# Ninth half rows of two weight matrices laid on the lower 64 partitions, in transfers of eight partitions

## The chip, the core and the metric

The kernel runs on one core of one Trainium2 chip. The metric is the device time of one execution in microseconds (us). Three runs of the kernel before took 2691.22, 2691.80 and 2693.41 us; their median is 2691.8 us. One further execution was profiled.

## The reference

The reference decodes one token for a batch of two through four blocks: attention, gated MLP, attention, gated MLP, each with a layer norm before it and the residual added after it. Both attention blocks use the same weights and the same cache, and so do both MLP blocks.

```python
# x (2, 1, 576); H = 32 heads, 8192 cached positions, head size 128; gate and up 576 x 4608
q = (ln(x) @ wq).reshape(B, 1, H, 128)
scores = einsum("bhqd,bhkd->bhqk", q, k_cache) * 128 ** -0.5
x = x + (einsum("bhqk,bhkd->bhqd", softmax(scores), v_cache)) @ wo
x = x + (gelu(ln(x) @ w_gate) * (ln(x) @ w_up)) @ w_down
# ... and both once more
```

All values are float32. The key and value caches are 268 MB each and are read once per attention block, apart from what the first block leaves in SBUF; `wq` is 9.4 MB, `w_gate` and `w_up` are 10.6 MB each.

## The kernel before, in words

**Items.** An attention block goes through 64 items: 60 pairs of heads of one batch entry, and four single heads. The keys of a pair lie on 128 partitions, 64 KB on each, and come as one transfer; so do its values. VectorE multiplies keys by the query (L554), GpSimd adds the two halves of each product (L574), VectorE sums the rest (L577), and TensorE multiplies the softmax weights with the values (L670). Block 0 goes up through the items, block 1 comes back down.

**Memory.** All keys, values and weights lie in one SBUF tile, `space`, 50,176 floats on each partition. `Arena` places them when the program is written. `plan_first`, `plan_mlp` and `plan_second` put the loads in one fixed list, and `pump` emits a load as soon as its place in the arena is free. All these loads are issued by one queue, SP, in that order, so a load that waits holds back all behind it.

**Counters.** The layer that turns the kernel into a program gives the transfers eight completion counters in turn. A transfer that takes a counter is not issued before the former transfer on the same counter has landed, so no more than eight are under way. It also puts a wait where a transfer writes to a part of a tile that an earlier instruction still uses.

**Half rows.** `wq`, and the gate and up matrices of the second MLP, are read by half rows. A matrix of 576 rows has 1152 half rows; partition p holds the nine half rows 9p to 9p+8, so a transfer of three of them is one run in DRAM on each partition. A half row of `wq` is 8192 bytes, one of the gate matrix 9216. The first `wq` and the second gate each come as three transfers of three half rows (`three`, L293). `norm` makes the matching left operand: one transpose on VectorE (L487) writes to `xt`, which has 32 columns for each of the nine half rows; TensorE then multiplies `xt` with `w` (L505 for `wq`, L843 for gate and up), one group of matmuls for each half row.

**The start.** SP issues the three transfers of the first `wq`, then K0 (the keys of the first pair), K1 and V0. The input `x` comes in eight small transfers of two partitions each from the queue of ScalarE (L140). The first multiplication on VectorE needs q, thus all of `wq`, and K0.

**The end.** After the last value products SP issues the eight transfers of `wo`, three of the gate matrix, five of the up matrix and seven of the down matrix; the last down products and the output store follow.

Of the kernel before, what the change touches and what calls it, by code (L numbers as in the profile page):

```python
# [9 lines left out]
F32 = mybir.dt.float32  # L10
# [5 lines left out]
P = 128  # L16
B = 2
H = 32
SK = 8192
DH = 128  # L20
# [5 lines left out]
HALF = P // 2  # L26

GH = 4
NU = 9
EQ = 512  # L30
HG = DF // 16
PAD = 6
# [8 lines left out]
NPLACE = 4  # L41
RING = 5 * SLOT
END = RING + NPLACE * PLACE
HELD = 5


# [21 lines left out]
class Arena:  # L68
# [38 lines left out]
    def fit(self, key, n, lo=0):  # L107

        for at in [self.at, lo] + sorted(end for _, end in self.live.values()):
            if lo <= at and at + n <= END and self.take(key, at, n) is not None:  # L110
                self.at = at + n
# [11 lines left out]
def decode_layers(ctx, tc, x_in, kc, vc, wq, wo, wg, wu, wd, out):  # L123
    nc = tc.nc
    scale = DH ** -0.5

    consts = ctx.enter_context(tc.tile_pool(name="consts", bufs=1))
    work = ctx.enter_context(tc.tile_pool(name="work", bufs=2))
    once = ctx.enter_context(tc.tile_pool(name="once", bufs=1))
    psum1 = ctx.enter_context(tc.tile_pool(name="psum1", bufs=1, space=PSUM))  # L130
    ctx.enter_context(tc.manual_schedule())

    space = consts.tile([P, END], F32, name="space")

    x = consts.tile([P, CW], F32, name="x")
    nc.vector.memset(x, 0.0)
    for c in range(4):
        for s in range(2):
            lo = 32 * c + s * B
# [69 lines left out]
    def weights(key, n, first, transfers):  # L209

        def make():
            at = arena.ring(key, n) if first is None else arena.fit(key, n, first)
            if at is None:
                return False
            t = ready[key] = part_at(at, n)
            transfers(t)
            return True

        queue.append(make)

    def half_rows(key, w, us, first):

        width = w.shape[1] // 2
        rows = w.rearrange("r (s w) -> (r s) w", w=width).rearrange("(p u) w -> p u w", p=P)

        def transfers(t):
            nc.sync.dma_start(t.rearrange("p (u w) -> p u w", w=width), rows[:, us[0]:us[-1] + 1, :])

        weights(key, len(us) * width, first, transfers)

    def split_rows(name, w, h, u):

        rows = w[:, DF // 2 * h:DF // 2 * (h + 1)].rearrange("(m r) w -> m r w", r=NU)

        def transfers(t):
            for e in range(2):
                nc.sync.dma_start(t[e::2, :], rows[:, 5 * e + u, :])

        weights((name, 0, h, u), DF // 2, None, transfers)
# [51 lines left out]

    single = [range(u, u + 1) for u in range(NU)]
    three = [range(u, u + 3) for u in range(0, NU, 3)]  # L293
    WQ = [three, single]
    GU = [three, three[:-1] + single[-3:]]

    DOWN = [
        [[(t, i) for i in range(lo, lo + 4)] for t in range(NT) for lo in (0, 4)] + [[(t, NI - 1) for t in range(NT)]],
# [12 lines left out]
    def plan_first():  # L311
        def k(n, *at):
            cache(name("k", 0, n), kc, n, *at)

        def v(n, *at):
            cache(name("v", 0, n), vc, n, *at)

        for us in WQ[0]:
            half_rows(("wq", 0, us[0]), wq, us, END - NU * H * DH // 2)
        last = PAIRS - 1  # L320
        k(0)
        for n in range(1, PAIRS):
            k(n)
            v(n - 1)
        k(SINGLE[0], (0,))
        half(("v", 0, last), vc, last, 0, 1)
        half(("v", 0, last), vc, last, 4, 5)
        k(SINGLE[1], (3,))
        v(SINGLE[0], (4,))

        k(SINGLE[2], (2,))
        products()
        k(SINGLE[3], (0,))
        v(SINGLE[1], (4,))
        v(SINGLE[2], (3,))
        for g in groups(0)[:2]:
            out_rows(0, g)
        v(SINGLE[3], (1,), (1,) * 4)
        for g in groups(0)[2:]:
            out_rows(0, g)  # L340
# [34 lines left out]
    def plan_mlp(layer):  # L375
        if layer == 0:
            for h in range(2):
                for u in range(4):
                    split_rows("g", wg, h, u)
                split_middle(h)  # L380
                for u in range(4):
                    split_rows("u", wu, h, u)
        else:
            for g, (name, w) in enumerate((("g", wg), ("u", wu))):
                for us in GU[g]:
                    half_rows((name, layer, us[0]), w, us, 0)
        for rows in DOWN[layer]:
            down(layer, rows)

# [20 lines left out]
    diag = consts.tile([P, 4], F32, name="diag")  # L410
    of = consts.tile([P, B], F32, name="of")
    both = ident.rearrange("p (c v b r) -> p b r v c", c=4, v=4, b=B)[:, :, :, 0, :]
    eight = consts.tile([P, B, 4], F32, name="eight")
    nc.vector.reduce_sum(eight, both, axis=AX.X)
    nc.vector.tensor_add(diag, eight[:, 0, :], eight[:, 1, :])
    nc.vector.reduce_sum(of, eight, axis=AX.X)
# [18 lines left out]

    xt = consts.tile([P, PAD + NU * 32], F32, name="xt")
    nc.vector.memset(xt, 0.0)


    acc = psum1.tile([P, 2, 512], F32, name="acc")
# [16 lines left out]
        return smalls[0][0:p, 0:n]  # L459


    def norm(split=False):
        stats = work.tile([P, 6], F32, name="stats")
        nc.vector.bn_stats(stats, x)
        apart = work.tile([P, 4, 6], F32, name="apart")
        nc.vector.tensor_mul(
            apart, stats.unsqueeze(1).to_broadcast([P, 4, 6]), strip.unsqueeze(2).to_broadcast([P, 4, 6])
        )
        every4 = small(P, 4 * 6)
        nc.tensor.matmul(every4, same, apart.rearrange("p c t -> p (c t)"), start=True, stop=True)  # L470
        mv = work.tile([P, 2], F32, name="mv")
        nc.vector.bn_aggr(mv, every4)
        xc = once.tile([P, CW, 2], F32, name="xc", tag="xc")
        xr = x.rearrange("p (m r) -> p r m", r=NU)
        xs = xc.rearrange("p w s -> p (w s)")
        if split:
            xm = xs[:, :5 * 32].rearrange("p (u m e) -> p u m e", u=5, e=2)
            parts = [(xm[:, 0:4, :, e], xr[:, 5 * e:5 * e + 4, :], 0) for e in range(2)]
            parts += [(xm[:, 4, :, e], xr[:, 4, :], e) for e in range(2)]
            xs = xs[:, :5 * 32].rearrange("p (u q) -> p u q", u=5)  # L480
        else:
            parts = [(xc[:, :, s], x, s) for s in range(2)]
            xs = xs.rearrange("p (q u) -> p u q", u=NU)
        for to, of_x, s in parts:
            nc.vector.tensor_scalar(to, of_x, mv[:, 0:1], side[:, s:s + 1], op0=ALU.subtract, op1=ALU.mult)
        u = xs.shape[1]
        nc.vector.transpose(xt[:, PAD:PAD + 32 * u].rearrange("p (u q) -> p u q", u=u), xs)  # L487
        ve = work.tile([P, 1], F32, name="ve")
        nc.vector.tensor_scalar_add(ve, mv[:, 1:2], EPS)  # L489
        rstd = work.tile([P, 1], F32, name="rstd")  # L490
        nc.gpsimd.tensor_tensor(out=rstd, in0=ve, in1=mhalf, op=ALU.pow)  # L491
        return rstd
# [3 lines left out]


    def attention(layer):
        rstd = norm()

        for us in WQ[layer]:
            w = ready.pop(("wq", layer, us[0])).rearrange("p (u c w) -> p u c w", c=4, w=EQ)
            for u in us:
                for c in range(4):
                    nc.tensor.matmul(  # L505
                        acc[32 * c:32 * c + 2 * B, 0, :], xt[:, PAD + 32 * u:PAD + 32 * u + 2 * B],
                        w[:, u - us[0], c, :], start=(u == 0), stop=(u == NU - 1),
                    )
            done(("wq", layer, us[0]))
        qsb = once.tile([P, EQ], F32, name="qsb", tag="row")  # L510
# [231 lines left out]
        for i, n in enumerate(seq):  # L742
            last = i == N - 1
            p = seq[i - 1] if i else None

            v = {N - 2: None, N - 1: N - 3}.get(i, i - 1) if layer == 0 else i - 1
# [3 lines left out]
            first = layer == 1 and i == 1  # L750
# [39 lines left out]
        n, p = seq[-1], seq[-2]  # L790
        add_up(n, ITEMS[n].parts - 1)
        first, second = groups(layer)[:2]
# [17 lines left out]

    def mlp(layer):
        split = layer == 0
        rstd = norm(split)
        hT = once.tile([P, 2, NI, 2, 2, B], F32, name="hT", tag="xc")

        def window(u, at):

            return xt[:, PAD + 32 * u - at:PAD + 32 * u - at + 4 * B]
# [16 lines left out]
        def all_products():  # L835

            for g, name in enumerate("gu"):
                for us in GU[g]:
                    w = ready.pop((name, layer, us[0])).rearrange("p (u v c w) -> p u v c w", v=2, c=4, w=HG)
                    for u in us:  # L840
                        for v in range(2):
                            for c in range(4):
                                nc.tensor.matmul(  # L843
                                    acc[32 * c:32 * c + 4 * B, v, :HG], window(u, 4 * g), w[:, u - us[0], v, c, :],
                                    start=(g == 0 and u == 0), stop=(g == 1 and u == NU - 1),
                                )
                    done((name, layer, us[0]))
# [25 lines left out]
        for rows in DOWN[layer]:  # L873
            w = ready.pop(("d", layer, rows[0])).rearrange("p (i c) -> p i c", c=D)
            for k, (t, i) in enumerate(rows):
                v, e = divmod(t, 2) if split else (t % 2, t // 2)
                for c in range(4):
# [3 lines left out]
                        start=(rows is DOWN[layer][0] and k == 0), stop=(t, i) == (NT - 1, NI - 1),  # L881
# [39 lines left out]
```

## Time and profile before

| What | Value |
|---|---|
| median of three runs | 2691.8 us (2691.22 to 2693.41) |
| profiled execution | 2693.42 us |
| its span | 2691.6 us |
| moved by DMA | 1154.36 MB, mean 429 GB/s |
| busy: VectorE, GpSimd, TensorE, ScalarE | 69%, 45%, 34%, 5% of the span |

The profiled execution's own time is 1.8 us more than its span, and 1.6 us over the median. The profile gives a line for each queue of the DMA engines (q1 is SP's, q10 ScalarE's, q8 and q14 fetch instructions), the chain of work that ended last, and on request the busy share of the 16 DMA engines and the bytes per second in any stretch of time. A stretch counts a packet's time and bytes in the slice where the view puts the packet, so a short stretch can show a share over 1.

### The profile page before, as it was taken

To read this page: it belongs to the slowest core of one execution; us is meant where nothing else is said; L and a number is where in the kernel's file an instruction comes from. 1 tells how busy PE (TensorE), PEld (TensorE's weight loads), DVE (VectorE), ACT (ScalarE), POOL (GpSimd) and SP (SyncE) were. 2 spreads that over 40 slices of the span, in tenths; PEclk is the share of its full clock that TensorE was granted. 3 is DMA by queue.
4 is the path that set the end of the run, shared out by engine and by line. 5 is a ranking of instruction groups with operands and counts; after the bars stand their busy time and mean duration, and the time that the engine had idled before them with its cause. 6 is when DMAs were issued, how large, how long until landed. Compare 5 with 4: busy or idle time off the path is not lost.

```text
span 2691.6 us, 18179 instructions
## 1 busy us (share of the span) xinstructions
PE 919.8 (34%) x7020; PEld 302.3 (11%) x7020; DVE 1850.8 (69%) x1688; ACT 145.6 (5%) x736; POOL 1213.8 (45%) x550
## 2 busy tenths in 40 slices
PE   1323332333233233334554232233233323332355
PEld 0100010000001010111211110001000100010022
DVE  4877787678677776867028777768767867787740
ACT  0000000000000000000016000000000000000000
POOL 2644454455445444544018554445444544454420
PEclk7656655665666566666756665666566556656667
DMA  9999999999999999999999999999999999999998
GB/s 421 436 435 434 433 431 435 429 435 434 432 435 433 434 433 429 433 429 426 407 397 416 435 434 436 434 430 436 430 433 434 435 432 433 436 433 430 430 426 374
DMA packets 33687, 1154.36 MB, mean 429 GB/s; under 512 B 4008, under 2 KB 4032, under 8 KB 5824
## 3 DMA queue, kind: packets, MB, share of 16 engines
q1 hardware_dynamic: 33560, 1153.19, 99.6%
q8 instruction: 55, 0.90, 0.1%
q14 instruction: 32, 0.26, 0.0%
q10 hardware_dynamic: 40, 0.01, 0.0%
HBM read 1153.18 MB, written 0.00 MB: 428 GB/s over the span
## 4 chain that ended last, share of the span: by engine, by line
DMA 79%; PE 12%; DVE 7%; POOL 1%; issue 1%; ACT 0%; SPq 0%; ACTq 0%; POOLq 0%; DVEq 0%
DMA space<-in_A_k_cache_dram 40%; DMA space<-in_A_v_cache_dram 32%; PE acc L670 10%; DVE space L554 4%; DMA space<-in_B_w_down_dram 2%; DVE S L577 2%; DMA space<-in_B_w_gate_dram 2%; DMA space<-in_A_wo_dram 1%; DMA space<-in_B_w_up_dram 1%; POOL space L574 1%; DMA space<-in_A_wq_dram 1%; PE bank L878 0%; PE acc L829 0%; POOL space L561 0%; DMA x<-in_A_x_dram 0%
## 5 line engine op out<-in xcount | busy, mean ns | idle before, releaser
L574 POOL TENSOR_TENSOR space<-space 128x1024 f32<-128x1024 f32 (+1 forms) x510 | 1180.7, 2315 | 1206.1 <-DVE space L554 1195.3
L554 DVE TENSOR_TENSOR space<-space,bank 128x2048 f32<-128x2048 f32 (+1 forms) x512 | 1153.6, 2253 | 604.7 <-DMA space<-in_A_k_cache_dram 576.5
L670 PE MATMUL acc<-space,prz 128*8 128x512 f32 x4096 | 594.3, 744 | 454.5 <-DMA space<-in_A_v_cache_dram 450.4
L577 DVE TENSOR_REDUCE S<-space 128x16 f32<-128x1024 f32 (+1 forms) x512 | 609.6, 1191 | 3.2 <-POOL space L574 3.0
L525 PE MATMUL bank<-qsb,pick 4*64 4x128 f32 (+1 forms) x256 | 47.0, 439 | 777.9 <-DVE space L554 765.6
L670 PEld LDWEIGHTS acc<-space,prz 128*8 128x8 f32 x4096 | 118.5, 104 | 873.4 <-DMA space<-in_A_v_cache_dram 452.7
L629 ACT ACTIVATE nbs<-bank 64x1 f32<-64x1 f32 (+1 forms) x128 | 21.2, 165 | 2258.6 <-PE bank L608 2257.7
L525 PEld LDWEIGHTS bank<-qsb,pick 4*64 4x64 f32 (+1 forms) x256 | 21.1, 203 | 836.7 <-DVE space L554 794.3
L695 PE MATMUL bank<-of,osb 128*32 128x2 f32 x512 | 40.9, 202 | 130.9 <-DVE osb L686 130.9
L608 PE MATMUL bank<-m,unit 1*128 1x2 f32 (+1 forms) x136 | 39.2, 355 | 129.5 <-DVE m L606 129.5
L491 POOL TENSOR_TENSOR rstd<-ve,mhalf 128x1 f32<-128x1 f32 x4 | 2.2, 550 | 168.6 <-DVE ve L489 168.6
L686 DVE SCALAR_TENSOR_TENSOR osb<-acc,diag,osb 128x128 f32<-128x128 f32 x192 | 67.3, 351 | 6.8
L640 PE MATMUL bank<-sums,unit 128*128 128x2 f32 x120 | 35.2, 363 | 92.2 <-ACT prz L631 92.2
L854 DVE STREAM_TRANSPOSE o<-o 128x288 f32<-128x288 f32 x4 | 2.8, 689 | 91.8 <-ACT o L852 91.8
L631 ACT ACTIVATE prz<-S,nbs 64x128 f32<-64x128 f32 (+1 forms) x128 | 50.7, 396 | 12.4 <-POOL prz L621 8.3
L695 PEld LDWEIGHTS bank<-of,osb 128*32 128x32 f32 x512 | 35.7, 154 | 139.1 <-DVE osb L686 137.9
L608 PEld LDWEIGHTS bank<-m,unit 1*128 1x128 f32 x136 | 33.3, 303 | 149.2 <-DVE m L606 149.2
L600 PE MATMUL bank<-ident,m 128*1 128x128 f32 x68 | 25.0, 368 | 72.0 <-DVE m L598 72.0
L495 DVE TENSOR_TENSOR x<-bank,x 128x144 f32<-128x144 f32 x4 | 1.2, 308 | 69.9 <-PE bank L878 40.9
L567 ACT ACTIVATE space<-space 128x128 f32<-128x128 f32 x164 | 48.5, 297 | 12.9 <-DVE space L554 7.4
L561 POOL TENSOR_TENSOR space<-space,qs 128x512 f32<-128x512 f32 x24 | 30.4, 1268 | 30.8 <-ACT qs L560 30.8
L640 PEld LDWEIGHTS bank<-sums,unit 128*128 128x128 f32 x120 | 30.0, 310 | 97.3 <-ACT prz L631 97.3
(68 smaller groups left out, 380.9 us busy)
## 6 DMA issues: line engine op xcount, KB each, us to landing
space<-in_A_v_cache_dram SPq DMA_DIRECT2D x8, 4096.0 KB
space<-in_A_k_cache_dram SPq DMA_DIRECT2D x6, 4096.0 KB
space<-in_A_wo_dram SPq DMA_DIRECT2D x15, 1152.0 KB
space<-in_A_k_cache_dram SPq DMA_DIRECT2D x15, 1024.0 KB
space<-in_B_w_gate_dram SPq DMA_DIRECT2D x3, 3456.0 KB
space<-in_A_v_cache_dram SPq DMA_DIRECT2D x10, 1024.0 KB
space<-in_A_wq_dram SPq DMA_DIRECT2D x3, 3072.0 KB
space<-in_B_w_gate_dram SPq DMA_DIRECT2D x16, 576.0 KB
```

Of the source, the lines that this page charges most:

```text
L525: nc.tensor.matmul(qb[n][to, :], pick[32 * c:32 * c + 4, r:r + 1].to_broadcast([4, P // it.heads]), qsb[32 * c:32 * c + 4, (h % 4) * DH:(h ...
L554: nc.vector.tensor_tensor(out=u[:, :rows, :], in0=t[:, :rows, :], in1=qb[n].unsqueeze(1).to_broadcast([P, rows, DH]), op=ALU.mult)
L561: nc.gpsimd.tensor_tensor(out=u[:, rows:, :], in0=t[:, rows:, :], in1=q.unsqueeze(1).to_broadcast([P, JC - rows, DH]), op=ALU.mult,)
L567: nc.scalar.activation(u[:, j, :], u[:, j, :], AF.Copy, accum_out=S[n][:, k * JC + j:k * JC + j + 1])
L574: nc.gpsimd.tensor_tensor(out=half, in0=half, in1=u[:, :r, DH // 2:], op=ALU.add)
L577: nc.vector.tensor_reduce(out=S[n][:, k * JC:k * JC + own_rows(n, k)], in_=prod.pop((n, k)), axis=AX.X, op=ALU.add)
L608: nc.tensor.matmul(mT[n][:, :heads], ones[0:1, :], m1[:, :heads], start=True, stop=True)
L631: nc.scalar.activation(pr[at, lo:].rearrange("p (g e) -> p g e", e=4)[:, 0:it.rows // 2:2, :], s[at, :it.rows].rearrange("p (g r) -> p g r ...
L640: nc.tensor.matmul(tot[:, :it.heads], ones, rs.pop(n), start=True, stop=True)
L670: nc.tensor.matmul(accumulator(n)[32 * c:32 * c + 8, :], pr[:, at:at + 8], t[g // 4][:, g % 4 * 4:g % 4 * 4 + 4, :].rearrange("p j d -> p ...
L686: nc.vector.scalar_tensor_tensor(t, q[:, r, :], diag[:, r:r + 1], t, op0=ALU.mult, op1=ALU.add,)
L695: nc.tensor.matmul(po[lo:lo + 32, i, :], t[:, i::GH], of, start=True, stop=True)
```

## The change

Of the first `wq` and of the second gate matrix, the ninth half row (u = 8) of the partitions 64 to 127 no longer goes to those partitions. It goes to the partitions 0 to 63, behind their own ninth half row. So the lower 64 partitions hold ten half rows and the upper 64 hold eight. The third transfer now brings two half rows to all 128 partitions; the ninth half rows, 64 on either side, come in eight further transfers. Each of them writes to eight partitions, every fourth one of 32 (0, 4, ..., 28, then 1, 5, ..., 29, and so on), and brings two half rows to each.

The left operand gets a second transpose, of the ninth group of rows 64 to 127, to columns of its own on the lower 64 partitions of `xt`. The matmuls of the ninth and of the new tenth half row run over 64 rows instead of 128: four more matmul calls for `wq`, eight more for the gate. In the arena both matrices take ten half rows instead of nine. The small tile `eight` moves to a shared buffer to make room.

```diff
+LOWER = range(NU - 1, NU + 1)
...
+    def lower_rows(key, w, first):
+
+        width = w.shape[1] // 2
+        rows = w.rearrange("r (s w) -> (r s) w", w=width).rearrange("(e p u) w -> p e u w", e=2, u=NU)[:, :, NU - 1, :]
+
+        def transfers(t):
+            t = t.rearrange("p (e w) -> p e w", w=width)
+
+            for lo in range(0, HALF, 32):
+                for j in range(4):
+                    at = slice(lo + j, lo + 32, 4)
+                    nc.sync.dma_start(t[at], rows[at])
+
+        weights(key, 2 * width, first, transfers)
...
-    WQ = [three, single]
-    GU = [three, three[:-1] + single[-3:]]
+
+    uneven = three[:-1] + [range(6, 8), LOWER]
+    WQ = [uneven, single]
+    GU = [uneven, three[:-1] + single[-3:]]
...
-            half_rows(("wq", 0, us[0]), wq, us, END - NU * H * DH // 2)
+            first = END - (NU + 1) * H * DH // 2
+            if us is LOWER:
+                lower_rows(("wq", 0, us[0]), wq, first)
+            else:
+                half_rows(("wq", 0, us[0]), wq, us, first)
...
-    eight = consts.tile([P, B, 4], F32, name="eight")
+    eight = once.tile([P, B, 4], F32, name="eight", tag="part")
...
-    xt = consts.tile([P, PAD + NU * 32], F32, name="xt")
+    xt = consts.tile([P, PAD + (NU + 1) * 32], F32, name="xt")
...
+        if lower:
+            nc.vector.transpose(xt[:HALF, PAD + 32 * NU:], xs[HALF:, NU - 1, :])
...
+            k = HALF if us is LOWER else P
             for u in us:
                 for c in range(4):
                     nc.tensor.matmul(
-                        acc[32 * c:32 * c + 2 * B, 0, :], xt[:, PAD + 32 * u:PAD + 32 * u + 2 * B],
-                        w[:, u - us[0], c, :], start=(u == 0), stop=(u == NU - 1),
+                        acc[32 * c:32 * c + 2 * B, 0, :], xt[:k, PAD + 32 * u:PAD + 32 * u + 2 * B],
+                        w[:k, u - us[0], c, :], start=(u == 0), stop=(u == WQ[layer][-1][-1]),
                     )
```

The gate products of the second MLP are changed in the same way as the last hunk.

More of the change, by code (lines that the diff above doesn't have):

```diff
@@ L385, in plan_mlp @@
                 for us in GU[g]:
-                    half_rows((name, layer, us[0]), w, us, 0)
+                    if us is LOWER:
+                        lower_rows((name, layer, us[0]), w, 0)
+                    else:
+                        half_rows((name, layer, us[0]), w, us, 0)
         for rows in DOWN[layer]:
@@ L459, in small, with norm @@
         return smalls[0][0:p, 0:n]
-    def norm(split=False):
+    def norm(split=False, lower=False):
         stats = work.tile([P, 6], F32, name="stats")
@@ L498, in attention @@
     def attention(layer):
-        rstd = norm()
+        rstd = norm(lower=LOWER in WQ[layer])
         for us in WQ[layer]:
             w = ready.pop(("wq", layer, us[0])).rearrange("p (u c w) -> p u c w", c=4, w=EQ)
+            k = HALF if us is LOWER else P
             for u in us:
@@ L812, in mlp @@
         split = layer == 0
-        rstd = norm(split)
+        rstd = norm(split, lower=not split and LOWER in GU[0])
         hT = once.tile([P, 2, NI, 2, 2, B], F32, name="hT", tag="xc")
@@ L839, in all_products @@
                     w = ready.pop((name, layer, us[0])).rearrange("p (u v c w) -> p u v c w", v=2, c=4, w=HG)
+                    k = HALF if us is LOWER else P
                     for u in us:
@@ L843, in all_products @@
                                 nc.tensor.matmul(
-                                    acc[32 * c:32 * c + 4 * B, v, :HG], window(u, 4 * g), w[:, u - us[0], v, c, :],
+                                    acc[32 * c:32 * c + 4 * B, v, :HG], window(u, 4 * g)[:k], w[:k, u - us[0], v, c, :],
                                     start=(g == 0 and u == 0), stop=(g == 1 and u == NU - 1),
```

## The prediction

> **What bounds the kernel now.** I read the page first, then the timelines of the start and the end, and then short stretches for the share of the DMA engines.
>
> ```profile
> span 2691.6 us, 18179 instructions
> DMA  9999999999999999999999999999999999999998
> GB/s 421 436 435 434 433 431 435 429 435 434 432 435 433 434 433 429 433 429 426 407 397 416 435 434 436 434 430 436 430 433 434 435 432 433 436 433 430 430 426 374
> q1 hardware_dynamic: 33560, 1153.19, 99.6%
> q8 instruction: 55, 0.90, 0.1%
> q14 instruction: 32, 0.26, 0.0%
> q10 hardware_dynamic: 40, 0.01, 0.0%
> DMA 79%; PE 12%; DVE 7%; POOL 1%; issue 1%; ACT 0%; SPq 0%; ACTq 0%; POOLq 0%; DVEq 0%
> L554 DVE TENSOR_TENSOR space<-space,bank 128x2048 f32<-128x2048 f32 (+1 forms) x512 | 1153.6, 2253 | 604.7 <-DMA space<-in_A_k_cache_dram 576.5
> ```
>
> The 16 DMA engines are busy in every slice, SP's queue alone fills 99.6% of their time, and the chain that ended last is 79% DMA. VectorE sits idle for 604.7 us ahead of its multiplications, nearly all of it (576.5) for keys. So the kernel is a stream of loads, and compute fits beside it. Time can come from two places only: engines that stand still, and engines that carry more than their share.
>
> The start, SP first, then the waits that follow:
>
> ```profile
> 0.74 7.10 SPq L227 DMA_DIRECT2D space<-in_A_wq_dram  x3
> 9.38 13.54 SPq L165 DMA_DIRECT2D space<-in_A_k_cache_dram  x2
> 9.36 0.02 issue
> 9.38 35.00 DMA space<-in_A_k_cache_dram
> 20.67 9.33 PE L505 MATMUL acc<-space,xt 128*4 128x512 f32 x72 [1.74 <-DVE ve L489]
> 44.47 2.29 DVE L554 TENSOR_TENSOR space<-space,bank 128x2048 f32<-128x2048 f32 x1 [23.82 <-DMA space<-in_A_k_cache_dram]
> ```
>
> K0 is issued at 9.38, long before the 9.4 MB of wq are through (at 434 GB/s, the usual slice of the GB/s row, they take 21.7 us). So K0's bytes follow wq's without a gap, and K0 lands at 9.38 + 35.00 = 44.38. The wq products end at 30.00 and have 14 us to spare.
>
> The end:
>
> ```profile
> 2594.28 5.90 SPq L227 DMA_DIRECT2D space<-in_B_w_gate_dram  x3
> 2602.64 11.43 SPq L227 DMA_DIRECT2D space<-in_B_w_up_dram  x5
> 2638.35 4.69 PE L843 MATMUL acc<-space,xt 128*8 128x288 f32 x48 [3.42 <-DMA space<-in_B_w_gate_dram]
> 2646.55 3.10 PE L843 MATMUL acc<-space,xt 128*8 128x288 f32 x48 [3.52 <-DMA space<-in_B_w_up_dram]
> 2638.37 43.25 DMA space<-in_B_w_down_dram
> 2687.92 0.47 PE bank L878 x8
> ```
>
> Gate's last third is there at 2638.35, up's first at 2646.55, and the last down rows at 2687.92, 3.7 us before the end of the span.
>
> How many engines are still at work just before that (columns: stretch, busy time by engine, granted clock, DMA share, GB/s):
>
> ```profile
> 2683.00:2684.00 1.00, 1.00 (x24) 0.72 (x20) 0.00 (x0) 0.00 (x0) 0.00 (x0) 0.50 0.58 240
> 2684.00:2685.00 1.00, 1.00 (x24) 0.72 (x20) 0.00 (x0) 0.00 (x0) 0.00 (x0) 0.50 0.54 217
> 2685.00:2686.00 1.00, 1.00 (x24) 0.70 (x18) 0.00 (x0) 0.00 (x0) 0.00 (x0) 0.50 0.22 90
> 2686.00:2687.00 1.00, 1.00 (x40) 0.75 (x28) 0.00 (x0) 0.00 (x0) 0.00 (x0) 1.00 0.17 69
> 2687.00:2688.00 1.00, 0.94 (x28) 0.40 (x24) 0.00 (x0) 0.00 (x0) 0.00 (x0) 1.00 0.08 26
> ```
>
> The engines do not end together. A share of 0.54 between 2684 and 2685 is 8.6 of 16 engines, so nine are at work there; then three or four, and one or two at the last. The last landing, on which the down products wait, is that of the slowest engine.
>
> **The change, part by part.** Bytes stay the same; what moves is which engines carry them, and when K0 may be issued. The sum is made on the profiled execution, 2693.42 us with a span of 2691.6; that is 1.6 over the median 2691.8, and I put the differences on the median.
>
> 1. *Half the engines carry the ninth half rows.* I take it that a transfer to eight partitions runs on eight of the 16 engines, the same eight each time. The nearest row is q10: its 40 packets come from ten small transfers, eight of x and two of the output, each of two rows, so four packets for each: two rows and two completion marks. A transfer of two rows thus does not go to 16 engines. The ninth half rows of wq are 128 x 8192 bytes = 1.05 MB. On 16 engines at 434 GB/s they take 2.42 us, on eight 4.83. Cost: 2.42. For gate, 128 x 9216 bytes = 1.18 MB: 2.72 and 5.44, cost 2.72. If they went to all 16 engines both costs would be nothing.
>
> [...]
>
> 2. *K0 waits for all eight small transfers.* In the built program K0's issue waits until every one of them has landed; before, it waited for a transfer of x alone, at 9.36. The partitions that they write to lie apart, and the layer below takes them as touching all of `space`. So after the last of them the engines run dry until K0's first bytes come. That restart shows at two places. At the very start wq is issued at 0.74; and late in the trace a key transfer is issued at 1415.74 to a queue nearly empty:
>
> ```profile
> 0.00:2.50 2.50, 0.00 (x0) 0.00 (x0) 1.20 (x10) 0.00 (x0) 0.70 (x6) 1.00 0.49 138
> 2.50:5.00 2.50, 0.00 (x0) 0.00 (x0) 2.17 (x9) 0.00 (x0) 0.00 (x0) 1.00 0.81 345
> 1415.74 0.33 SPq L165 DMA_DIRECT2D space<-in_A_k_cache_dram  x1
> 1416.00:1417.00 1.00, 0.00 (x0) 0.00 (x0) 1.00 (x1) 0.00 (x0) 0.17 (x1) 1.00 0.54 106
> 1417.00:1418.00 1.00, 0.00 (x0) 0.00 (x0) 1.00 (x3) 0.63 (x5) 0.59 (x1) 1.00 0.75 287
> 1418.00:1419.00 1.00, 0.00 (x0) 0.00 (x0) 1.00 (x1) 1.00 (x8) 1.00 (x2) 1.00 0.97 410
> ```
>
> 2.5 x 138 + 2.5 x 345 = 1208 KB by 5.00, worth 2.78 us at 434 GB/s; so it is as if the full rate began at 2.22, 1.48 after the issue. At the other place 106 + 287 + 410 = 803 KB are worth 1.85 us, full rate from 1417.15, 1.41 after the issue. I take 1.45. From a landing to the issue that waits for it the chain shows 0.02; with eight counters to pass I put 0.3. So K0's stream begins 2.42 + 1.45 + 0.3 = 4.2 us later. Below, if step 1 is nothing, 1.75 stays; above, if an engine falls behind by a further restart, 5.7. All that follows in the first attention waits for keys and values, so nothing takes this up again: 4.2.
>
> 3. *The tail.* The gate's eight transfers add 2.72 us to eight engines and take 2.72 from the others. If the slowest engine is among the eight, the end comes 2.72 later. If it isn't: nine engines are at work at 2684.5, so at least one of them is among the eight, and it ends no sooner than about 2685.3 + 2.72 = 2688.0 against 2687.9, so the tail is 0.1 later. No choice of eight makes the tail shorter. I take the upper value, 2.7: which engine is last has no row, but followed packet by packet the trace has q8's fetches by turns on eight streams, x's two rows on none of these, and the stream that ends last is none of these either; x's two engines and the eight partitions' engines should be of the same half.
>
> Behind the eight, up's first transfer is queued. The last small one waits for the counter of the gate's third transfer, now two half rows, 2638.35 - 2.72 = 2635.6; up's first waits for the first small one, 0.7 later, 2636.3, plus 1.45: 2637.8. The slow engine is busy with small transfers until 2635.6 + 5.4 = 2641.0, so it does not run dry; the other half does for up to 2.2 us, and pays with the 2.72 it was spared. SP has 8 more issues; it issued up's first at 2602.64 and now does so 34 us later, which is still before the bytes are wanted.
>
> 4. *The rest costs nothing while the cover lasts.* The second transpose is of 64 x 32:
>
> ```profile
> L487 DVE STREAM_TRANSPOSE xt<-xc 128x160 f32<-128x160 f32 x1 | 0.3, 345 | 0.0
> ```
>
> Under 0.35, twice. At the start it stands ahead of q, which has 14 us to spare; in the second MLP ahead of gate products that wait for the gate anyway. The wq products take 9.33/9 = 1.04 us for a half row, so after the last small transfer (about 27.5) two half rows end at 29.6, and K0 lands at 48.6. If that cover were gone they would cost 1 us. K1 still waits only for the first products, V0 for the last ones, near 30 as before, with K0 and K1 queued ahead. `eight` in the shared buffer is read before anything else takes it: nothing.
>
> Sum: 4.2 + 2.7 = 6.9 us; 2691.8 + 6.9 = 2698.7.
>
> **The rivals.**
> - *The tail is hidden* (the slowest engine is of the other half): 4.2 + 0.1, 2696.1. For it: eight streams carry the larger fetches, q8 with 0.90 MB against q14's 0.26. Against it: the last stream is not of them.
> - *The small transfers run on all 16 engines*, so the change doesn't do what it says: only the wait is left, 1.75, 2693.5. Against it: q10's packets.
> - *Not slower: the shift evens out the engines.* If the late ones were all of the upper half, 2.72 less on them would give back 2.7 at the tail, and 4.2 - 2.7 = 1.5: 2693.3. It decides once eight or fewer engines are at work after 2683; the share of 0.58 there says nine. Against K0's wait it would have to bring over 4.2 to be faster at all.
> - *Each small transfer pays a restart of its own*, 8 x 1.45 instead of one: 10 us more at the start, 2708.9. Against it, the transfers of 64 partitions in the first MLP:
>
> ```profile
> 1290.00:1310.00 20.00, 11.57 (x150) 4.49 (x154) 2.43 (x10) 0.00 (x0) 0.55 (x1) 0.83 1.01 397
> ```
>
> They keep 397 GB/s, since queued transfers overlap. [...]
>
> **How the numbers follow.** Forecast (4.2 and 2.7) 0.64; tail hidden 0.15; 16 engines 0.08; evened out 0.06; own restarts 0.07. What a measurement can tell from no change is 0.2%, 5.4 us: 2697.2 and above is slower. Slower: the forecast, the last rival and a fifth of the hidden tail, 0.74. Faster needs below 2686.4, which no case reaches unless it is off by 7: 0.04. Same: 0.22. The range leaves out the restarts and part of the two cases near 2693.4: from 2693.5 to 2702.0, which is 4.2 raised to 5.7 at the start, 2.7 at the tail, and the 1.6 by which single runs lie above the median. The forecast's own range is 2696.5 to 2701.
>
> **What would show it.** Right: K0 issued near 27.5 instead of 9.38, a dip in GB/s just behind it, VectorE's first multiplication near 48.7, and up's first products near 2646.55 + 6.9. Wrong: the first multiplication under 46.3 (16 engines) or over 51 (own restarts); or a tail, from gate's second third to the end, as long as before.

## The result, and the profile after

The changed kernel takes 2701.07 us (median of 7 runs, 2699.43 to 2702.44) against 2692.66 us for the kernel before, run beside it (7 runs, 2691.22 to 2693.41). The ratio is 1.0029, 95% interval 1.0019 to 1.0039: slower by 8.4 us. The forecast was slower by 6.9 us, to 2698.7 us, with a range of 2693.5 to 2702.0 us that holds the result. The two ends cost 5.45 and 2.8 us in the profile, where the forecast had 4.2 and 2.7.

The profiled execution has a span of 2700.0 us, 8.4 over that of before. Four lines of its page:

```profile
span 2700.0 us, 18259 instructions
DMA  9999999999999999999999999999999999999998
GB/s 389 436 433 433 434 433 431 434 432 433 432 434 433 434 433 430 433 429 424 406 399 412 440 433 431 431 434 435 433 430 433 435 434 430 432 433 431 434 423 359
L582 DVE TENSOR_TENSOR space<-space,bank 128x2048 f32<-128x2048 f32 (+1 forms) x512 | 1153.6, 2253 | 609.6 <-DMA space<-in_A_k_cache_dram 581.1
```

The first slice moves 389 GB/s instead of 421 and the last 359 instead of 374; the slices between are as before. VectorE waits 4.9 us longer ahead of its multiplications (609.6 against 604.7), for keys. So the loss lies at the two ends. The start, first the timelines of SP and VectorE and then the chain of waits:

```profile
9.56 13.95 SPq L243 DMA_DIRECT2D space<-in_A_wq_dram  x8
27.88 0.81 SPq L166 DMA_DIRECT2D space<-in_A_k_cache_dram  x2
49.92 2.29 DVE L582 TENSOR_TENSOR space<-space,bank 128x2048 f32<-128x2048 f32 x1 [28.62 <-DMA space<-in_A_k_cache_dram]
```

```profile
22.85 4.91 DMA space<-in_A_wq_dram
27.76 0.02 SPq L166
27.88 21.95 DMA space<-in_A_k_cache_dram
```

K0 is issued at 27.88 instead of 9.38, behind the landing of the last small transfer (22.85 + 4.91 = 27.76). It lands at 49.83, and the first multiplication starts at 49.92, 5.45 us later than before (44.47).

Short stretches of the start (columns as in the prediction: stretch, length, busy time by engine, granted clock, share of the 16 DMA engines, GB/s):

```profile
22.00:24.00 2.00, 2.00 (x12) 0.30 (x8) 0.00 (x0) 0.00 (x0) 0.00 (x0) 1.00 0.48 201
24.00:26.00 2.00, 2.00 (x16) 0.40 (x12) 0.00 (x0) 0.00 (x0) 0.00 (x0) 1.00 0.53 221
26.00:28.00 2.00, 2.00 (x24) 0.39 (x16) 0.00 (x0) 0.00 (x0) 0.00 (x0) 1.00 0.18 74
```

While the small transfers run, half of the engines are busy (0.48, 0.53), each at its usual pace: 221 GB/s over 0.53 of 16 engines is 26 GB/s for one, and 434 over 16 is 27. The share alone would also fit sixteen engines that are busy half the time, but the packets in the trace speak against that: between 22 and 26 us eight of them, for moments nine, are under way at any time, and each one of 8192 bytes takes 309 ns. Then the engines run nearly dry until K0 comes.

The end, SP and TensorE:

```profile
2608.42 33.62 SPq L243 DMA_DIRECT2D space<-in_B_w_gate_dram  x8
2642.15 3.01 SPq L228 DMA_DIRECT2D space<-in_B_w_up_dram  x5
2627.82 5.92 PE L872 MATMUL acc<-space,xt 128*8 128x288 f32 x48 [4.50 <-DMA space<-in_B_w_gate_dram]
2647.32 4.02 PE L872 MATMUL acc<-space,xt 64*8 64x288 f32 x32 [3.81 <-DMA space<-in_B_w_gate_dram]
2655.13 5.92 PE L872 MATMUL acc<-space,xt 128*8 128x288 f32 x48 [3.78 <-DMA space<-in_B_w_up_dram]
2696.51 0.47 PE bank L907 x8
```

I call the time from gate's first products to up's first products "the gate's time": 2655.13 - 2627.82 = 27.31 us. Before, gate's first products stood at 2622.03:

```profile
2622.03 5.95 PE L843 MATMUL acc<-space,xt 128*8 128x288 f32 x48 [4.51 <-DMA space<-in_B_w_gate_dram]
```

so it was 2646.55 - 2622.03 = 24.52. From up's first products to the last down products both kernels take 41.4 us (2696.51 - 2655.13, 2687.92 - 2646.55). In these two executions the change costs 5.8 us until the gate comes, 2.8 us at the gate, and nothing after it.

### The profile page after: what moved, and what is told of

The parts are those of the page before. It is cut to its first block, busy times and chain, and to the rows that moved or that the text cites. A ratio compares the mean times of both kernels' runs of the same rounds, so it can differ in the third digit from the quotient of the medians.

```text
span 2700.0 us, 18259 instructions
## 1 busy us (share of the span) xinstructions
PE 925.2 (34%) x7044; PEld 302.0 (11%) x7044; DVE 1851.7 (69%) x1690; ACT 145.6 (5%) x736; POOL 1214.5 (45%) x550
## 4 chain that ended last, share of the span: by engine, by line
DMA 80%; PE 11%; DVE 7%; POOL 1%; issue 1%; ACT 0%; SPq 0%; ACTq 0%; POOLq 0%; DVEq 0%
DMA space<-in_A_k_cache_dram 39%; DMA space<-in_A_v_cache_dram 32%; PE acc L698 10%; DVE space L582 4%; DMA space<-in_B_w_down_dram 2%; DVE S L605 2%; DMA space<-in_B_w_gate_dram 2%; DMA space<-in_B_w_up_dram 1%; DMA space<-in_A_wq_dram 1%; DMA space<-in_A_wo_dram 1%; POOL space L602 1%; POOL space L589 0%; PE bank L907 0%; DMA x<-in_A_x_dram 0%; PE acc L533 0%
## 5 line engine op out<-in xcount | busy, mean ns | idle before, releaser
L582 DVE TENSOR_TENSOR space<-space,bank 128x2048 f32<-128x2048 f32 (+1 forms) x512 | 1153.6, 2253 | 609.6 <-DMA space<-in_A_k_cache_dram 581.1
```

The source lines that it names most:

```text
L582: nc.vector.tensor_tensor(out=u[:, :rows, :], in0=t[:, :rows, :], in1=qb[n].unsqueeze(1).to_broadcast([P, rows, DH]), op=ALU.mult)
```

## The experiments

All eleven, beside the two kernels. "First product" is the start of VectorE's first multiplication, "gate" the gate's time, both from the one profiled execution; the loss is the median minus that of the kernel before, run beside it (2692.66 us for the changed kernel; 2693.47 for 1 to 4, 2693.31 for 5 to 8, 2693.28 for 9 to 11), with the ratio's 95% interval.

| Kernel | first product | gate | loss, us | ratio, interval |
|---|---|---|---|---|
| before | 44.47 | 24.52 | | |
| changed | 49.92 | 27.31 | 8.4 | 1.0019 to 1.0039 |
| 1 wq alone | 49.53 | 24.52 | 5.0 | 1.0011 to 1.0029 |
| 2 gate alone | 44.61 | 27.36 | 2.5 | 0.9999 to 1.0016 |
| 3 adjacent partitions | 56.15 | 36.31 | 21.9 | 1.0069 to 1.0097 |
| 4 four transfers of 16 | 49.76 | 30.44 | 10.4 | 1.0026 to 1.0051 |
| 5 one transfer of 64 | 47.85 | 33.72 | 12.6 | 1.0036 to 1.0061 |
| 6 on the upper half | 49.86 | 33.03 | 13.0 | 1.0036 to 1.0062 |
| 7 adjacent places only | 57.05 | 36.25 | 22.9 | 1.0073 to 1.0100 |
| 8 every eighth of 64 | 53.97 | 34.24 | 20.2 | 1.0064 to 1.0095 |
| 9 wq in one, gate in eight | 47.92 | 27.35 | 5.6 | 1.0011 to 1.0029 |
| 10 gate alone, 16 higher | 44.62 | 33.49 | 8.4 | 1.0020 to 1.0043 |
| 11 adjacent source rows only | 50.02 | 26.79 | 7.9 | 1.0018 to 1.0040 |

### 1 and 2: one place at a time

```diff
# 1
-    GU = [uneven, three[:-1] + single[-3:]]
+    GU = [three, three[:-1] + single[-3:]]
# 2
-    WQ = [uneven, single]
+    WQ = [three, single]
```

> Only the first wq is changed, the second gate is as before. Theory (the two places add, and each is paid in full): the first K lands 5.5 us later than before, as in the changed kernel, nothing later gives it back, and the time is that of before plus 5.5, about 2698.2. Rival (what comes late at the start is made up during the streaming, and all 8.4 us are from the tail): within 1 us of before, about 2693.

> Only the second gate is changed, the first wq is as before. Theory (the eight partitions' engines hold the slowest one, and it ends last): the start is as before, up's first products come 2.8 us later, and the time is that of before plus 2.8, about 2695.5. Rival (the tail's loss in the changed kernel is only what the start's disorder of the engines left behind): up's first products no later than before, time within 0.5 us of it.

Measured: 2698.45 and 2696.01 us, 5.0 and 2.5 over before. The first product of kernel 1, then gate's and up's first products of kernel 2:

```profile
49.53 2.29 DVE L582 TENSOR_TENSOR space<-space,bank 128x2048 f32<-128x2048 f32 x1 [28.59 <-DMA space<-in_A_k_cache_dram]
2622.10 5.95 PE L872 MATMUL acc<-space,xt 128*8 128x288 f32 x48 [4.47 <-DMA space<-in_B_w_gate_dram]
2649.46 5.95 PE L872 MATMUL acc<-space,xt 128*8 128x288 f32 x48 [3.78 <-DMA space<-in_B_w_up_dram]
```

The two losses add to 7.5 of the 8.4, and each sits at its own end: kernel 1 has the late first product and the old gate's time, kernel 2 the reverse. Neither rival holds. For kernel 2 the time alone would not say so, since its interval (0.9999 to 1.0016) holds 1, which is no change. The gate's time does: it is 24.52 us in the two kernels with the old gate (before and 1), and 26.79 to 27.36 us in the four with the new one in the changed kernel's places (changed, 2, 9, 11). In kernel 1's profiled execution the gate's first products are only 3.56 us late (2625.59) where the first product was 5.06 late; that execution took 2696.80 us, 1.65 under its median, so the streaming between moves a single execution by such an amount and is not part of the change.

### 3 and 4: another cut of the same bytes

```diff
# 3: eight adjacent partitions
-            for lo in range(0, HALF, 32):
-                for j in range(4):
-                    at = slice(lo + j, lo + 32, 4)
-                    nc.sync.dma_start(t[at], rows[at])
+            for lo in range(0, HALF, 8):
+                at = slice(lo, lo + 8)
+                nc.sync.dma_start(t[at], rows[at])
# 4: sixteen, every fourth of 64
+            for j in range(4):
+                at = slice(j, HALF, 4)
+                nc.sync.dma_start(t[at], rows[at])
```

> Both changed, but each of the eight transfers takes eight adjacent partitions instead of every fourth of 32. Theory: the first K no longer waits until all eight have landed and is issued near 23.5 us; what is left at the start are the eight engines, 2.4 us by the bytes, and the tail is as in the changed kernel, 2.8: about 5.2 over before, 2697.9, and about 3.1 under the changed kernel. Rival A (the small transfers themselves cost the start, not the wait behind them): as the changed kernel, 8.4 over before, 2701.1. Rival B (the engine follows the partition's place, and every fourth partition was what kept to eight engines): all the loss but the wait goes, 2693 to 2696.

> Both changed, but the 64 partitions come in four transfers of 16 (every fourth of 64) instead of eight of 8; the first K still waits for all four. Theory (as many engines as partitions, up to sixteen): no stretch of the start is at half rate, the wait is left with its restart, 2.5 to 3 us at the start, and nothing at the tail: 2.5 to 3 over before, about 2695.4. Rival (the engines are set by something else than the number of partitions): half rate stays and with it all of it, 2701.1.

Measured: 2715.41 and 2703.85 us, both over every value expected, kernel 3 by 14 us. Kernel 3's K0 was indeed issued earlier (25.39 instead of 27.88), and still the first product came 6.2 us later than in the changed kernel. The same stretches tell why, kernel 3 first, then kernel 4:

```profile
22.00:24.00 2.00, 2.00 (x12) 0.30 (x8) 0.00 (x0) 0.00 (x0) 0.00 (x0) 1.00 0.57 82
24.00:26.00 2.00, 2.00 (x16) 0.41 (x12) 0.00 (x0) 0.00 (x0) 0.00 (x0) 1.00 0.50 82
```

```profile
22.00:24.00 2.00, 2.00 (x16) 0.40 (x12) 0.00 (x0) 0.00 (x0) 0.00 (x0) 1.00 1.09 258
24.00:26.00 2.00, 2.00 (x24) 0.48 (x20) 0.00 (x0) 0.00 (x0) 0.00 (x0) 1.00 1.03 209
```

In kernel 3 half the engines are busy, but they move 82 GB/s together, 10 each. In kernel 4 all sixteen are busy and move 209, 13 each. In the trace eight packets are under way together in kernel 3 and sixteen in kernel 4, and a packet of 8192 bytes takes some 630 ns in kernel 4 instead of 309. So in these kernels the number of partitions does set the number of engines (eight and eight, sixteen and sixteen), but more engines bring nothing here: the 1.05 MB go from 21.7 to 27.1 us in kernel 4 and from 21.6 to 27.4 us in the changed kernel. Something else shares out about 210 GB/s, and far less, 82, when the eight partitions are neighbours. That gave the new theory, written ahead of kernel 5: what counts is which places of SBUF are written.

### 5 and 8: more engines on the lower half, and places wider apart

```diff
# 5 (in place of the changed kernel's loops)
+            nc.sync.dma_start(t[:HALF], rows)
# 8 (in place of the changed kernel's loops)
+            for j in range(8):
+                at = slice(j, HALF, 8)
+                nc.sync.dma_start(t[at], rows[at])
```

> Both changed, but each ninth comes in one transfer of 64 partitions; the first K waits for none of it. New theory (places: the runs so far show 309 ns for 8 KB with eight engines on every fourth of 32 partitions, 586 ns with sixteen engines on every fourth of 64, 844 ns on eight adjacent partitions, so places that lie next to each other, or 32 apart, take from one rate): the 64 lower partitions take half the full rate whatever the engines, so the start keeps 2.4 us by the bytes but loses the wait's part, and V and the first gate come 2.4 later where the four transfers of 16 had 3.6; the tail keeps 2.7 by the bytes, up to 5.9 as with the four transfers of 16. Sum 5.1 to 8.3 over before, 2698.6 to 2701.8. Rival (the engines are all that counted, and the four transfers of 16 were slow by their stride alone): all sixteen at full rate and no wait, within 1 us of before, 2693 to 2694.5. [...]

> Both changed, eight transfers of every eighth of the 64 partitions instead of every fourth of 32. [...] Rival (only partitions next to each other collide): as the changed kernel, 2701.

Kernel 8 first: 2713.54 us, nowhere near the rival.

```profile
22.00:24.00 2.00, 2.00 (x16) 0.39 (x12) 0.00 (x0) 0.00 (x0) 0.00 (x0) 1.00 0.55 131
24.00:26.00 2.00, 2.00 (x24) 0.39 (x17) 0.00 (x0) 0.00 (x0) 0.00 (x0) 1.00 0.48 98
26.00:28.00 2.00, 2.00 (x24) 0.48 (x20) 0.00 (x0) 0.00 (x0) 0.00 (x0) 1.00 0.53 131
28.00:30.00 2.00, 1.23 (x12) 0.10 (x4) 0.00 (x0) 0.00 (x0) 0.00 (x0) 1.00 0.50 102
```

Eight engines on every eighth of 64 partitions move 98 to 131 GB/s where every fourth of 32 gave 201 to 221. No two of these partitions are neighbours, so it isn't adjacency alone. In the changed kernel partitions 4 to 28 apart ran side by side at the usual pace, 26 GB/s for each engine, so by these two kernels it should be those 32 or more apart that share a rate; 32 is the one distance that gives each of the eight a partner, which fits the 12 to 16 GB/s of each engine here (98 and 131 over eight). This is inferred from the rates: no record names the place of a packet. The first product is 9.5 us late, and the gate's time is 9.7 us longer.

Kernel 5 takes 2705.91 us, over the 2698.6 to 2701.8 expected. Its start does what the theory says in kind:

```profile
10.39 14.40 SPq L166 DMA_DIRECT2D space<-in_A_k_cache_dram  x2
22.00:24.00 2.00, 2.00 (x12) 0.30 (x8) 0.00 (x0) 0.00 (x0) 0.00 (x0) 1.00 1.05 225
24.00:26.00 2.00, 2.00 (x20) 0.41 (x16) 0.00 (x0) 0.00 (x0) 0.00 (x0) 1.00 1.04 213
47.85 2.29 DVE L579 TENSOR_TENSOR space<-space,bank 128x2048 f32<-128x2048 f32 x1 [26.61 <-DMA space<-in_A_k_cache_dram]
```

All engines are busy at half the rate, K0 is issued at 10.39 without waiting for the 64 rows, and the first product is 3.4 us late. Nor is 64 partitions a slow number in itself: the row at 1290 us that the prediction shows, with 397 GB/s at a share of 1.01, has transfers of 64 partitions too, but those are every second one of all 128. Against kernel 4, which has the same sixteen engines and the wait (49.76), the wait is worth 1.9 us. What the theory missed is the gate: its time is 9.2 us longer than before, where the theory had 2.7 by the bytes at half rate and 5.9 at most.

### 7 and 11: the places written, or the rows read

Kernel 7 has the changed kernel's source rows with kernel 3's places, kernel 11 the reverse. In both the ninth half rows lie on other partitions than the products take them for, so the output is not the reference's; the work is the same.

```diff
# 7
-                    nc.sync.dma_start(t[at], rows[at])
+                    nc.sync.dma_start(t[lo + 8 * j:lo + 8 * j + 8], rows[at])
# 11
+                    nc.sync.dma_start(t[at], rows[lo + 8 * j:lo + 8 * j + 8])
```

> As the changed kernel, with the same source rows in each transfer (every fourth of 32), but written to eight adjacent partitions, so that the ninth half rows lie on other partitions than the products take them for: the output is not the reference's, the work is the same. Theory (the places written set the rate): as with adjacent partitions on both sides, 20 to 23 over before, about 2715. Rival (the rows read in HBM set it): as the changed kernel, 2701, or less as the first K does not wait, 2698.

> The counterpart of the run with adjacent places: eight adjacent source rows in each transfer, written to every fourth of 32 partitions, so that rows lie on other partitions than the products take them for and the output is not the reference's; the work is the same. Theory (only the places written count): as the changed kernel, 8.4 over before, about 2701.5. Rival (adjacent rows in HBM cost too): between that and 2715.

Measured: 2716.21 and 2701.18 us, each as the theory said within 1.3 us. A stretch of kernel 7, then the same of kernel 11:

```profile
24.00:26.00 2.00, 2.00 (x16) 0.44 (x12) 0.00 (x0) 0.00 (x0) 0.00 (x0) 1.00 0.50 78
```

```profile
24.00:26.00 2.00, 2.00 (x20) 0.40 (x16) 0.00 (x0) 0.00 (x0) 0.00 (x0) 1.00 0.53 221
```

Which rows are read makes no difference that shows (7.9 us over before against 8.4); which partitions are written makes 15 us.

### 6 and 10: the same pattern, moved

Kernel 6 mirrors the change: the lower half's ninth rows lie on partitions 64 to 127. Kernel 10 changes the gate alone, as kernel 2 does, and writes 16 partitions higher, while its products still read partitions 0 to 63.

```diff
# 6 (transpose, matmul rows and columns mirrored to match)
-                    nc.sync.dma_start(t[at], rows[at])
+                    nc.sync.dma_start(t[HALF:][at], rows[at])
# 10 (wq as in kernel 2)
-                    nc.sync.dma_start(t[at], rows[at])
+                    nc.sync.dma_start(t[16 + lo + j:48 + lo:4], rows[at])
```

> Both changed and mirrored: the ninth half rows of the lower 64 partitions lie on the upper ones, in the same eight transfers of every fourth of 32, the second transpose and the products mirrored with them. Theory (eight partitions are carried by the same eight engines wherever they lie, and the upper half takes half the rate like the lower): as the changed kernel, start 5.5, tail 2.8, about 2701. Rival (the place picks the engines, so that the upper places go to the other eight, which do not hold the slowest): the start as before it, the tail 0 to 1, about 2698 to 2699.

> Only the second gate is changed, in eight transfers of every fourth partition, but these start 16 partitions higher: partitions 16 to 47 and 48 to 79 instead of 0 to 31 and 32 to 63. The products still read 0 to 63, so the output is not the reference's; the work is the same. Theory Q (the eight engines of such a transfer write, from partition 0 on, to the rates that they use in every whole transfer too, and so disturb nobody; 16 higher, each writes where another engine is writing): up's first products later by more than the 2.8 us of the unrotated one, by 4 to 9, the range from four transfers of 16 to the upper places: 2697 to 2702. Rival (any eight places with eight rates are alike): 2.8 as before, 2696.

Kernel 6: 2706.31 us, 13.0 over before; both the theory (2701) and the rival (2698 to 2699) are wrong. Its start is that of the changed kernel (first product 49.86; 193 and 217 GB/s at a share of 0.50 and 0.52). The difference is in the gate's time, 33.03 against 27.31. There, other transfers are still under way when the small ones run. The stretch of the gate in which the two kernels differ most in pace, the changed kernel first:

```profile
2636.00:2640.00 4.00, 4.00 (x44) 1.56 (x48) 0.00 (x0) 0.00 (x0) 0.00 (x0) 0.62 0.62 263
```

```profile
2636.00:2640.00 4.00, 2.39 (x40) 0.88 (x32) 0.00 (x0) 0.00 (x0) 0.00 (x0) 1.00 0.84 173
```

The changed kernel moves 263 GB/s at a share of 0.62, which is the full pace of 424 for sixteen engines; kernel 6 moves 173 at 0.84, a pace of 206. Its engines are busy, and slow. The packets show it: the gate's whole third transfer has packets of 18,432 bytes and the small ones have 9216. In the changed kernel they take 686 and 347 ns side by side. In kernel 6 both take twice as long between 2636 and 2640 us (some 1420 and 720 ns), and the small ones are back at 347 ns between 2642 and 2644 us, when the whole transfer is all but through. So small and whole transfers slow each other there, and only while both run. That suggested theory Q, and kernel 10 was made for it: every fourth partition of 32 as before, only 16 higher. It took 2701.66 us, 8.4 over before where kernel 2 lost 2.5, and its gate's time is 6.1 us longer than kernel 2's:

```profile
2632.00:2636.00 4.00, 4.00 (x44) 1.30 (x36) 0.00 (x0) 0.00 (x0) 0.00 (x0) 0.60 0.64 150
2621.48 4.79 PE L872 MATMUL acc<-space,xt 128*8 128x288 f32 x48 [5.44 <-DMA space<-in_B_w_gate_dram]
2654.97 5.11 PE L872 MATMUL acc<-space,xt 128*8 128x288 f32 x48 [3.47 <-DMA space<-in_B_w_up_dram]
```

150 GB/s at 0.64 is a pace of 234, and again both kinds of packet take about twice as long side by side (some 1340 and 700 ns between 2632 and 2634 us). So the rival (any eight places are alike) falls. That the two kinds slow each other is in the records; they do not name the engine or the place of a packet, so that the small transfers' engines write where other engines of the whole transfer write is inferred. It also fits kernels 4 and 5, which write to the lower half alone with all sixteen engines (shares of 1.03 to 1.09 at the start), and where both kinds of packet are slow as well (some 1420 and 730 ns from 2634 us to 2636); why 5 loses 3.3 us more than 4 at the gate stays open.

### 9: the wait taken away

```diff
         def transfers(t):
+            if first:
+                nc.sync.dma_start(t[:HALF], rows)
+                return
```

Here `first` is set for `wq` and 0 for the gate, so `wq` has kernel 5's cut and the gate the changed kernel's.

> The first wq's ninth in one transfer of 64 partitions, as in the run before (no wait of the first K), the second gate's in the changed kernel's eight transfers. Theory (start and tail add, each with the price its own cut had): the first multiplication of VectorE near 47.85, as with 64 partitions, 3.4 later than before, and up 2.8 later by the tail: 6.2 over before, 2699.5. Rival (the one transfer's high total came from its start, which leaves the engines apart until the end): the gate's thirds and up as late as with 64 partitions at both places, 2703 to 2706.

Measured: 2698.83 us, first product 47.92, gate's time 27.35: within 0.7 us of the theory in all three, so the prices of start and end add. The loss is 5.6 us where the changed kernel's was 8.4. No cut beat the kernel before.

## Why the prediction was right, point by point

**What bounds the kernel: right.** The loss is in the first and the last slice; TensorE's and VectorE's new instructions show in neither end's chain.

**Step 1, half the engines: right, but for half of the reason.** Half the engines carry the small transfers (0.48 and 0.53), and the one sentence that hung on it, "If they went to all 16 engines both costs would be nothing", is wrong. Kernels 4 and 5 did go to all sixteen, and lost 10.4 and 12.6 us. The bound is double: eight partitions bring eight engines, and the 64 lower partitions take some 210 GB/s from eight engines (201 and 221) and from sixteen (209 to 225, but for one stretch of 258 in kernel 4). Both halve the rate, so the term came out right, and that is luck: the prediction knew only the first. The rival "all 16 engines" priced the engines alone, and 2693.5 us was not to be had.

That eight partitions bring eight engines was the author's assumption when the sum was made; the runs show it: shares of 0.48 and 0.53 with eight packets under way for eight partitions, 1.03 and 1.09 with sixteen packets for sixteen (kernel 4), 1.04 and 1.05 for 64 (kernel 5). Which eight of the sixteen they are stands in no record. The bound on the places has no row in the profile of before; the runs of kernels 4, 5 and 8 showed it, in kernel 8 with 98 to 131 GB/s from eight engines on every eighth partition.

**Step 2, K0 waits: right in kind, with one term missing and one too small.** K0's issue was put near 27.5 and came at 27.88. From issue to landing K0 takes 21.95 us; its 8.39 MB at 434 GB/s are 19.33, which leaves 2.6 us where the prediction had 1.45. Two things are in this.

First, the restart itself. The prediction read it from stretches that count a packet whole where it starts, and so the engines seem to fill sooner than they do. With each packet's bytes spread over its time, the first `wq` reaches the full rate as if 1.73 us after its issue instead of 1.48, and K0 in the changed kernel as if after 1.84. So the restart was put 0.4 too low.

Second, a landing comes later than the bytes at an even pace would end, since the engines don't end together and the landing follows the last data (K0's last data come at 49.49, its landing at 49.83). The kernel before pays this once, for K0. The changed kernel pays it twice, because K0 also waits for the landing of the last small transfer: at an even pace all of `wq` would be through at 0.74 + 1.73 + 19.33 + 4.83 = 26.63 us (issue, restart, eight half rows of each partition at 434 GB/s, the ninth ones at half of that), and the landing is at 27.76. This wait of 1.1 us has no term in the sum.

Together the start is 2.42 for the bytes, 1.13 to the landing (put at nothing), 0.12 from there to the issue (put at 0.3) and 1.84 for the restart (put at 1.45), 5.5 us by this working and 5.45 as measured. It stayed inside the bounds given (1.75 to 5.7), whose upper one was there for another reason, an engine that falls behind by a restart. Taking the wait away gives back less than the last three of these: 1.9 us between kernels 4 and 5, 2.0 between the changed kernel and kernel 9, whose cut of `wq` differs too. Even without it kernel 5 starts 3.4 us late, 1.0 more than its bytes at half rate; this was not taken further apart.

**"Nothing takes this up again": right** as far as the medians tell: `wq` alone costs 5.0 us (3.0 to 7.8 by the interval) for a first product 5.06 us late. One execution can drift by 1.5 us on the way, as kernel 1 showed.

**Step 3, the tail: right.** 2.8 us against 2.7, at the place named: up's first transfer was put at 2636.3, plus the start's 5.8 us that is 2642.1, and it was issued at 2642.15. So the slow engine is among the eight. The packets of the changed kernel show it: the last 18,432-byte packet of the gate's third transfer ends at 2640.85 us, 2.0 us after the last of all the others (2638.87), a 9216-byte packet starts at once, and sixteen of them at 347 ns end at 2646.40. The prediction had this as one of two cases and took it on an argument, that x's two engines and the eight are of one half; that was the author's estimate, and no run shows it. Kernels 6 and 10 show that the tail also hangs on where the eight write (a gate's time of 33.03 and 33.49 us), which the prediction did not ask. The other half stood still from 2638.87 at the latest until up's first packets at 2643.27, so 4.4 us where the prediction allowed 2.2. It cost nothing, since that half had been spared 2.72 us and was 2.0 ahead of the slow engine.

**Step 4, nothing else: right.** Kernel 2 has the longer `norm` and the 64-row products of the gate, and loses 2.5 us, no more than the gate's eight transfers. At the start the products of `wq` end at 32.2 instead of 29.6 and V0 is issued at 32.22 instead of near 30, still 17 us before K0 lands.

**The rivals.** The tail hidden and evened out: fell with kernel 2 (27.36). Sixteen engines: fell with the changed kernel's own shares of 0.48 and 0.53, and kernels 4 and 5 show that its price would not have held with sixteen. Own restarts: fell with the first product at 49.92, under the 51 set for it.

## What to carry to other kernels

A transfer to part of the partitions had two limits here, its engines (eight for eight partitions, 201 and 221 GB/s) and the places that it writes (209 to 225 GB/s from sixteen engines on the lower 64, but for one stretch of 258), and to lift one did nothing while the other held; read the DMA share and the GB/s of a short stretch together, since here a share of 0.53 with 221 GB/s, the usual pace for each engine, meant few engines, and a share of 1.03 with 209 GB/s meant that something behind the engines was shared. Before moving rows to one half of SBUF, estimate its price from these runs: at least its bytes at half rate (2.42 us more for 1.05 MB here), plus 2 to 3 us wherever the next load now waits for it to land (without the wait 1.9 and 2.0 us came back; the changed kernel's start cost 3.0 beyond its bytes). A restart read from stretches that count packets whole where they start came out too short (1.48 against 1.73 us for the first `wq`). Where such a transfer ran beside whole ones, its place mattered as well as its size: 16 partitions higher cost another 6 us.

## What the hardware showed that I had not expected

- Eight adjacent partitions in each of eight queued transfers: 70 to 82 GB/s, against 201 to 221 for every fourth of 32, with eight packets under way in both, and whatever rows are read (kernels 3, 7 and 11).
- Sixteen engines on the lower 64 partitions: 209 to 225 GB/s but for one stretch of 258, and 1.05 MB in 5.4 to 5.9 us against 5.8 with eight (kernels 4 and 5).
- The same eight-partition pattern costs the gate 2.8 us on partitions 0 to 63, 8.5 on the upper half, and 9.0 when moved up by 16 (kernels 2, 6 and 10), though at the start, where next to nothing runs beside it, lower and upper places cost the same (first product 5.45 and 5.39 late). Where it costs more, its packets and those of the whole transfer beside it take twice as long.
